# Wider zero products in TensorE's idle time, and a new order for an attention and Fourier-mixing kernel

## The chip, the cores and the metric

The kernel runs on one core of a Trainium2 chip. The core has five engines that work side by side, each through its own queue in order: TensorE (PE; its weight loads are listed as PEld), VectorE (DVE), ScalarE (ACT), GpSimd (POOL) and SyncE (SP), which only issues transfers. The metric is the device time of one execution in microseconds (us), the median over runs. The profile is of one execution and gives its span, from the first to the last instruction.

## The reference, cut to what matters

Chunked attention over four batches of eight heads, then a two-dimensional Fourier transform whose real part is added, a normalisation and a two-layer network with residual:

```python
# attention: q, k, v are (4, 8, 768, 64), mem_k and mem_v (4, 8, 8, 64)
for c in range(S // 32):                       # chunks of 32 queries
    k_ctx = k[:, :, l_start:r_end]             # 16 keys to the left, 8 to the right
    k_full = np.concatenate([mem_k, k_ctx], axis=2)
    v_full = np.concatenate([mem_v, v_ctx], axis=2)
    scores = scale * np.matmul(q_c, k_full.transpose(0, 1, 3, 2))
    a = softmax(scores)
    out[:, :, c_start:c_end] = np.matmul(a, v_full)
# x is (4, 768, 512): the heads side by side
X = np.fft.fft(np.fft.fft(x, axis=1), axis=2)
u = x + np.real(X)
un = (u - mu) / np.sqrt(var + 1e-06)
return u + np.maximum(un @ w_ch1, 0.0) @ w_ch2   # 512 x 2048 and 2048 x 512
```

## The kernel before, in words

Work is cut by batch (`b`, four) and by head pair (`n`, sixteen, four in each batch). For a head pair, q and k are loaded by POOL (`e_load_qk`, L369), v by SP (`e_load_v`, L378 to L387) into the tiles `va`. TensorE transposes q and k in 16 small products each (`turn`, L397; results `trq`, `trk`); ACT copies `trq` out (L415), DVE copies `trk` into the key tile `kTb` (L440). Scores go out in two blocks of twelve products (L453), ACT makes the exponentials (L463), TensorE multiplies with v (L505, tiles `xa` and `xo`), and DVE divides by the sums into `xsb` (L515, L516). There is one bank for scores, so a second block waits for the exponential of the first.

The Fourier transform of a batch is made with tables of sines and cosines as matrix products: rows (L723 and L736 for the first batch, L577 for the others, tile `ps`), then columns (L747, L768, one last row L628, tile `pm`). The tables are made in the kernel: POOL counts (L315, L317), DVE makes angles (L1030 to L1038), ACT the sines (L1177 to L1181), then loads the table of the exponential (L1198). The network's first layer is L885 with the activation L894, its second L903 or, for most parts, L952, which saves products by sums of blocks that DVE makes (L940, tiles `S` and `w_t`) and adds with L957.

Of the first batch's four head pairs the transform needs them all: DVE's folds (L647, L658), POOL's sums of the middle column (L709 to L712, tile `mid`) and DVE's splits into two half-precision parts (L703) stand between the last values and the first row products. L717 is a zero product that clears a bank ahead of L723.

The order in every queue is not written out by hand. `add` records each piece of work as a task with an engine, a cost in microseconds, the tasks that it follows, the buffers that it takes and gives, and a rank. `Plan.order` then goes through planned time and places, on each engine that is free, the ready task of the lowest rank; the program is issued in that order. So a changed cost or rank moves instructions in the queues, on all engines, and semaphores alone decide when they run. `settled(moved)` overwrites the ranks of single tasks, by number, ahead of that.

Zero products: while TensorE is planned idle between the two tasks in `plan.filling`, `order` puts in `e_fill`, a product of the zero tile `dz` into a bank that is given back at the end of the stretch. `FILL` is the cost that is planned for one; TensorE costs count twice in planned time before `WARM`. `t_fill` places the first one. `make_identity` (POOL) and `e_idb` (DVE) make the identity that the transposes need.

Of the kernel before, what the change touches and what calls it, by code (L numbers as in the profile page):

```python
# [13 lines left out]
AFT = mybir.ActivationFunctionType  # L14
# [22 lines left out]
class Plan:  # L37
# [4 lines left out]
    LAG = {"PE": 0.2}  # L42
    OVER = {"DVE": 0.08, "ACT": 0.1}
    FIRST = 45.0
    WARM = 18.0
    SLACK = 0.7
    lead = 0
    ROOM = 1.15
    FILL = 0.17
    filling, fill = None, None  # L50

    def __init__(self, slots):
# [3 lines left out]
    def add(self, engine, cost, emit, after=(), take=(), give=(), rank=None, moved=0.0,  # L56
            loose=False, late=0.0, filler=False, behind=None, lag=0.0, pick=None, grain=0.1, head=1.0, dense=0.15):
        t = dict(engine=engine, cost=cost, emit=emit, after=[a for a in after if a is not None],
                 take=take, give=give, rank=len(self.tasks) if rank is None else rank,
                 moved=moved, done=None, at=None, no=len(self.tasks), loose=loose,  # L60
                 late=late, filler=filler, behind=behind, lag=lag, picks=[pick] if pick else [], grain=grain, head=head, dense=dense)
        self.tasks.append(t)
        return t
# [131 lines left out]
def kernel(  # L195
# [15 lines left out]
    P = 128  # L211
# [766 lines left out]
            nc.sync.dma_start(out[b, HS:HS + 1, :], od[b % 2, 0, 0:1, :])  # L978

    t_zero = add("DVE", 0.2, e_zero, rank=-21)  # L980
    t_table = add("ACT", 1.4, lambda: nc.scalar.activation(warm, zero, AFT.Sin), [t_zero], rank=-3)
    t_iota = add("POOL", 0.7, e_iota, rank=-5)
    t_mkf = add("ACT", 0.2, e_mkf, moved=2.04, grain=0.077, head=6.5)
    t_id = add("POOL", 0.5, lambda: make_identity(nc, ident), rank=-1.5)
    t_scales = add("DVE", 0.2, e_scales, [t_iota], rank=-19)
    t_ones = {}
    def e_idb():
# [4 lines left out]

    t_idb = add("DVE", 0.5, e_idb, [t_id], rank=-16.5)
    t_kz = add("DVE", 0.5, lambda: nc.vector.memset(ks[0][QP:KP], 0.0), rank=-16.95)
    t_kzs = add("POOL", 1.0, lambda: [nc.gpsimd.memset(ks[i][QP:KP], 0.0) for i in range(1, NS)],
                rank=14)
    t_low, LOW = {}, 110
    for i in range(NV):
        e_ = add("DVE" if i < 2 else "POOL", 0.45, lambda i=i: e_edges(i),
                 rank=(-20, -17.3, 17, 17)[i])  # L1000
        t_ones[i] = add("POOL", 0.7, lambda i=i: e_edge_ones(i), [e_], rank=(-3.5, 2, 17.1, 17.1)[i])
        t_low[i] = add("ACT", 1.45, lambda i=i: e_low_rows(i), [t_zero, e_],
                       rank=(0, 1, 2, 3)[i])
    t_masks = add("POOL", 0.86, e_masks, rank=16)
    dz = cpool.tile([P, P], BF16)
    fill_of = []
    t_dz = add("DVE", 0.15, lambda: nc.vector.memset(dz, 0.0), rank=-30)

    def e_fill():
        if not fill_of:  # L1010
            fill_of.append(bank("mlp", [P, 512], FP32, "idle"))
        nc.tensor.matmul(fill_of[0][:, 0:384], dz, strided(dz, 0, [[0, 3], [1, P]]),
                         start=True, stop=True)

    t_fill = add("PE", 0.33, e_fill, [t_dz], take=("mlp",), rank=-1)
    plan.fill = e_fill
    SINES = len(plan.tasks)
    t_kTz = [add("POOL", 0.45, lambda i=i: nc.gpsimd.memset(kTb[i][:, :, 0:MEM0], 0.0), rank=3)
# [5 lines left out]
    tabD = [(yD, rD, kk, sv[:, 0:1], svD[:, 0:1])]  # L1024
    t_angle = {}
    ANG = dict(S=-18, D=-10)
    for nm, parts, y, r, NN, c in (("S", tabS, yS.rearrange(fl3), rS.rearrange(fl3), S, 0.8),
                                   ("D", tabD, yD.rearrange(fl2), rD.rearrange(fl2), DM, 0.6)):

        t1 = [add("DVE", 0.37, lambda p_=p_: nc.vector.tensor_scalar(  # L1030
            p_[0], p_[2], p_[4], FSC, ALU.mult, ALU.add), [t_scales], rank=ANG[nm] + 0.1 * i)
            for i, p_ in enumerate(parts)]
        t2 = add("DVE", c, lambda y=y, NN=NN: nc.vector.tensor_scalar(
            y, y, FSC, float(NN), ALU.subtract, ALU.mult), t1, rank=ANG[nm] + 1)
        t3 = [add("DVE", 0.6 if nm == "S" else 0.75, lambda p_=p_: nc.vector.scalar_tensor_tensor(
            p_[1], p_[2], p_[3], p_[0], ALU.mult, ALU.subtract), [t2], rank=ANG[nm] + 2 + 0.1 * i)
            for i, p_ in enumerate(parts)]
        t_angle[nm] = add("DVE", c, lambda y=y, r=r: nc.vector.scalar_tensor_tensor(  # L1038
            y, r, -1.0, r, ALU.mult, ALU.max), t3, rank=ANG[nm] + 3)
# [160 lines left out]
        t_low[i]["behind"] = t_exp[i - 2, 1]  # L1200
        t_low[i]["rank"] = t_exp[i - 2, 1]["rank"] + 0.1
    t_neg = add("DVE", 0.6, e_negatives, [t_sines], rank=100)
    t_rows = add("DVE", 1.0, e_table_rows, [t_sines, t_neg], rank=101)
    t_idh = add("DVE", 0.25, lambda: nc.vector.tensor_copy(ident_h, ident), [t_id], rank=140)


# [14 lines left out]
    def first_fourier():  # L1221
        t_rest, t_mid, t_row, t_rows_, pre, seen, t_lo = {}, {}, {}, {}, {}, [], ([], [])
        both = None
        for g in range(2):
# [28 lines left out]
            for par in range(2):  # L1253
                for ab in range(2):
                    end = (ab, g) == (1, 1)
                    if g == 0:
                        ff = add("DVE", 0.5,
                                 lambda par=par, ab=ab, g=g: g_ff(par, ab, g, 1),
                                 [pre[par, ab, g], t_norm[3, g]])
                    else:  # L1260
                        ff = add("DVE", 0.55, lambda par=par, ab=ab: g_both(par, ab),
                                 pre[par, ab, 1][:2] + (seen + [pre[p, a, 1][2] for p in range(2) for a in range(2)]
                                                        if (par, ab) == (1, 1) else []),
                                 give=("dn",) if (par, ab) == (1, 1) else ())
                        seen.append(ff)
                    if (par, ab, g) == (0, 0, 1):
                        t_mark.append(ff)
                    hi = add("ACT", 0.5, lambda par=par, ab=ab, g=g: g_hi(par, ab, g),
                             [ff] + (pre[par, ab, 1][2:] if g == 1 else [pre[par, ab, 2]]),
                             take=(("hl",), ("hT",))[par] if (ab, g) == (0, 0) else ())  # L1270
                    lo = add("DVE", 0.48, lambda par=par, ab=ab, g=g: g_lo(par, ab, g),
                             [hi] + (t_lo[par] if end else []), give=("fold",) if end else ())
                    t_lo[par].append(lo)
                    if (par, ab, g) == (0, 0, 0):
                        plan.filling = (t_sc[0, 0], add("PE", 0.0, lambda: let_go(fill_of[0]), [lo],
                                                        give=("mlp",)))
                    tag = ("acc", "mlp")[par]
                    mid_ = (par, ab) == (0, 1)
                    rw = add("PE", 1.0, lambda par=par, ab=ab, g=g: g_rows(par, ab, g),
                             [lo, t_neg, t_rows_.get((par, ab))] + ([t_row[g]] if mid_ else [])  # L1280
                             + ([t_rows_[par, 0]] if end else []),
                             take=(tag,) if g == 0 and not mid_ else (),
                             give=(("hl",), ("hT",))[par] if end else ())
                    t_rows_[par, ab] = rw
                    if g == 1:
                        up = add("ACT", 0.6, lambda par=par, ab=ab: e_up(0, par, ab), [rw],
                                 take=("up",))
                        t_rest[par, ab] = add("DVE", 0.6,
                                              lambda par=par, ab=ab: e_rest(0, par, ab), [up],
                                              give=(tag,))  # L1290
# [260 lines left out]
    for b in range(B):  # L1551
# [3 lines left out]
    t_lv[15]["behind"] = t_x2[TURNED - 1]  # L1555

    moved = {
# [6 lines left out]
        262: 135.01, 269: 1.00059e+06, 275: 396.87, 280: 185.16, 290: -124.87, 318: -83.04, 359: 134.87,  # L1564
# [4 lines left out]
    }  # L1569
    with tc.manual_schedule():  # L1570
        for t in plan.settled(moved):
# [31 lines left out]
```

## Time and profile before

| | us |
|---|---|
| three runs | 276.18, 277.38, 277.41 |
| their median | 277.38 |
| the profiled execution | 276.81 |
| its span | 275.1 |
| TensorE busy | 258.2 (94%) |
| DVE busy | 206.1 (75%) |
| ACT busy | 160.3 (58%) |
| POOL busy | 80.4 (29%) |

A busy TensorE is not one at its peak, since matmuls are pipelined and their ends are modelled. In the timeline a line gives the start in microseconds, the time that the piece took, engine, source line, operation, the tile written and those read, shapes and the number of instructions; the bracket gives the idle time of the engine before it and what ended that. In the rows of merged products the time runs to the modelled end of the last one, so steps from one start to the next are the surer measure. The time of an execution is longer than its span by what lies around the first and last instruction, here 276.81 - 275.1 = 1.7 us.

### The profile page before, as it was taken

How to read it: one execution, taken by the hardware profiler on the slowest of the kernel's cores; microseconds unless marked ns; L12 is line 12 of the kernel's file. 1: busy time of each engine (PE TensorE's matmuls, PEld its weight loads, DVE VectorE, ACT ScalarE, POOL GpSimd, SP SyncE). 2: the span in 40 equal slices, each digit the busy share in tenths (PEclk: the TensorE clock that was granted, in tenths of full speed). 3: DMA queues.
4: the chain of work that ended last, by engine and by line, in shares of the span. 5: the costliest groups of instructions: out<-in, count | busy, mean ns of one | idle time of the engine just before them, and what ended most of it. 6: DMA issues, size and time to landing. Idle time of an engine off the chain costs nothing.

```text
span 275.1 us, 8156 instructions
## 1 busy us (share of the span) xinstructions
PE 258.2 (94%) x3365; PEld 211.5 (77%) x3365; DVE 206.1 (75%) x460; ACT 160.3 (58%) x300; POOL 80.4 (29%) x146
## 2 busy tenths in 40 slices
PE   0299999999999999999999989999999999999995
PEld 0278688788766679767768878888889889888884
DVE  7988997942336999899997996649998868444444
ACT  6598557777764779625935746737164374715150
POOL 8872382241111028025208346001100171100000
PEclk9999999999999999999999999999999999999999
DMA  6997999999999979994599967644942127313152
GB/s 107 202 182 121 175 157 206 197 196 197 195 185 240 235 100 239 170 153 113 186 165 250 176 101 134 141 92 163 133 166 38 41 50 164 89 49 76 66 89 76
DMA packets 116117, 39.98 MB, mean 145 GB/s; under 512 B 104560, under 2 KB 111472, under 8 KB 116080
## 3 DMA queue, kind: packets, MB, share of 16 engines
q1 hardware_dynamic: 93888, 23.54, 46.6%
q0 software_dynamic: 21472, 15.21, 33.8%
q10 hardware_dynamic: 720, 0.72, 0.8%
q8 instruction: 26, 0.43, 0.7%
q14 instruction: 11, 0.09, 0.1%
HBM read 37.36 MB, written 13.37 MB: 184 GB/s over the span
## 4 chain that ended last, share of the span: by engine, by line
PE 78%; DVE 13%; ACT 2%; DMA 2%; issue 2%; SPq 1%; POOL 1%; POOLq 0%; DVEq 0%
PE ph L885 25%; PE pc L952 14%; PE pc L903 10%; PE ps L577 6%; PE xa L505 5%; PE xo L505 3%; PE pm L747 3%; PE ps L736 3%; DVE S L940 2%; PE trk L397 2%; PE trq L397 2%; DMA va<-in_mem_v_dram 2%; DVE xsb L516 1%; PE sc L476 1%; PE sc L453 1%
## 5 line engine op out<-in xcount | busy, mean ns | idle before, releaser
L885 PE MATMUL ph<-unT,w_sb 128*128 128x256 f16 x768 | 89.3, 273 | 0.0
L885 PEld LDWEIGHTS <-w_sb 128*128 128x128 f16 x768 | 73.8, 98 | 10.1 <-issue 0.6
L894 ACT ACTIVATE hT<-ph 128x512 f16<-128x512 f32 x96 | 55.5, 600 | 40.9 <-PE ph L885 17.2
L952 PEld LDWEIGHTS <-hT 128*128 128x128 f16 x320 | 30.9, 98 | 4.7 <-issue 0.8
L952 PE MATMUL pc<-w_sb,hT 128*128 128x256 f16 x256 | 31.9, 273 | 0.3 <-DVE xsb L957 0.3
L957 DVE TENSOR_TENSOR xsb<-pc,xsb 128x256 f32<-128x256 f32 x57 | 23.6, 420 | 9.3 <-PE pc L952 7.9
L903 PE MATMUL pc<-w_sb,hT 128*128 128x512 f16 x128 | 29.7, 380 | 0.0
L488 ACT ACTIVATE e<-sc,mbias 128x192 f32<-128x192 f32 (+1 forms) x48 | 18.8, 491 | 5.4 <-PE sc L476 5.4
L903 PEld LDWEIGHTS <-hT 128*128 128x128 f16 x128 | 11.9, 98 | 12.9 <-issue 0.2
L940 DVE TENSOR_TENSOR S<-hT 128x768 f16<-128x768 f16 (+1 forms) x16 | 8.1, 506 | 16.6 <-ACT hT L894 16.3
L463 ACT ACTIVATE e<-sc,mbias 128x384 f32<-128x384 f32 x32 | 17.0, 581 | 3.6 <-PE sc L453 3.6
L820 DVE BATCH_NORM_STATS2 st<-xsb 128x6 f32<-128x512 f32 x24 | 16.6, 692 | 2.6 <-POOL xsb L808 2.0
L589 ACT CAST up<-ps 128x386 f16<-128x386 f32 x16 | 9.7, 608 | 13.6 <-PE ps L577 12.0
L834 ACT ACTIVATE un<-xsb,rs 128x512 f16<-128x512 f32 x16 | 12.6, 811 | 8.4 <-POOL rs L849 8.4
L952 PE MATMUL pc<-w_t,S 128*128 128x256 f16 x128 | 15.8, 273 | 1.3 <-DVE xsb L957 0.7
L808 POOL TENSOR_TENSOR xsb<-mix,xr 128x512 f32<-128x512 f32 x6 | 8.2, 1368 | 28.0 <-ACT mix L802 24.1
L505 PEld LDWEIGHTS xa<-va,e 128*64 128x64 f32 x384 | 13.1, 143 | 3.8 <-issue 3.0
L505 PE MATMUL xa<-va,e 128*64 128x65 f32 x384 | 15.4, 232 | 0.0
L952 PEld LDWEIGHTS <-S 128*128 128x128 f16 x128 | 12.4, 98 | 3.3 <-issue 1.1
L505 PE MATMUL xo<-va,e 128*64 128x65 f32 x384 | 14.2, 224 | 0.0
L369 POOL DMA_DIRECT2D qs<-in_q_dram x12 | 7.8, 651 | 21.8 <-PE trq L397 18.8
L620 POOL DMA_DIRECT2D xr<-x_back x3 | 2.3, 773 | 37.8 <-ACT up L589 14.2
(189 smaller groups left out, 488.7 us busy)
## 6 DMA issues: line engine op xcount, KB each, us to landing
va<-in_v_dram SPq DMA_DIRECT2D x32, 220.0 KB
w_sb<-in_moe_w_ch_dram POOLq DMA_DIRECT2D x8, 512.0 KB, 15.6
out_dram<-xsb SPq DMA_DIRECT2D x12, 256.0 KB
ks<-in_k_dram POOLq DMA_DIRECT2D x12, 192.0 KB, 6.2
qs<-in_q_dram POOLq DMA_DIRECT2D x12, 192.0 KB, 6.4
x_rows<-xsb POOLq DMA_DIRECT2D x3, 768.0 KB, 4.9
xr<-x_back POOLq DMA_DIRECT2D x3, 768.0 KB, 5.6
out_rows<-xsb SPq DMA_DIRECT2D x9, 256.0 KB
```

Source lines behind the costliest of these rows:

```text
L463: nc.scalar.activation(e1[:, :, :, ts(half, 32)], sc[:, :, 0:6, ts(half, 32)], AFT.Exp, bias=mbias[:, half:half + 1], scale=1.0 / math.sqr ...
L488: nc.scalar.activation(to, src, AFT.Exp, bias=mbias[:, half:half + 1], scale=1.0 / math.sqrt(D))
L505: nc.tensor.matmul(xa[64 * half:64 * half + 64, st, hh, 0:65], e1[:, hh, t6, :], v1[:, hh, 6 * g + t6, 0:65], start=True, stop=True)
L577: nc.tensor.matmul(out_[:, sp, :], part[:, ab, sp * 3 + st, c0:c1], tab[:, sp, st, :], start=(st == 0 and i == 0), stop=(st == 2 and i == 1))
L820: nc.vector.bn_stats(st6, xs[b][:, kt, :])
L834: nc.scalar.activation(un, xs[b][:, kt, :], AFT.Identity, bias=rs[:, 1:2], scale=rs[:, 0:1])
L885: nc.tensor.matmul(ph[:, k, :], w1_sb[:, dt, ts(HH * k + i, P)], unT_of[b, j][:, dt, :], start=(dt == 0), stop=(dt == NDT - 1))
L894: nc.scalar.activation(hT_of[b, j][:, :, i, :], ph, AFT.Relu, bias=0.0, scale=1.0 if (b, j) in FAST else -1.0)
L903: nc.tensor.matmul(pc_of[b, j, r], hT_of[b, j][:, k, i, ts(r, P)], w2_sb[:, HH * k + i, :], start=(i + k == 0), stop=(i + k == HH))
L940: nc.vector.tensor_tensor(out_[:, lo:hi], a[:, lo:hi], c[:, lo:hi], op)
L952: nc.tensor.matmul(pc_of[key], a[:, i, :], w[:, i, :], start=(i == 0 and new), stop=(i == HH - 1), skip_group_check=not new)
L957: nc.vector.tensor_tensor(u, pc, u, ALU.add)
```

## The change

The zero product is made 512 columns wide instead of 384, and its planned cost goes from 0.17 to 0.215 us. The stretch in which it may be placed begins with the first zero product itself instead of the first score block. The planner's `WARM`, up to which TensorE costs count twice, goes from 18 to 6 us of planned time. Costs of tasks of the first microseconds are set anew, and the list of overwritten ranks is replaced by another one of 74 entries. What is computed is the same.

```diff
-    WARM = 18.0
+    WARM = 6.0
...
-    FILL = 0.17
+    FILL = 0.215
...
-    t_table = add("ACT", 1.4, lambda: nc.scalar.activation(warm, zero, AFT.Sin), [t_zero], rank=-3)
+    t_table = add("ACT", 1.55, lambda: nc.scalar.activation(warm, zero, AFT.Sin), [t_zero], rank=-3)
...
-    t_mkf = add("ACT", 0.2, e_mkf, moved=2.04, grain=0.077, head=6.5)
-    t_id = add("POOL", 0.5, lambda: make_identity(nc, ident), rank=-1.5)
+    t_mkf = add("ACT", 1.3, e_mkf, moved=2.04, grain=0.077)
+    t_id = add("POOL", 0.7, lambda: make_identity(nc, ident), rank=-1.5)
...
-    t_kzs = add("POOL", 1.0, lambda: [nc.gpsimd.memset(ks[i][QP:KP], 0.0) for i in range(1, NS)],
+    t_kzs = add("POOL", 2.0, lambda: [nc.gpsimd.memset(ks[i][QP:KP], 0.0) for i in range(1, NS)],
                 rank=14)
...
-        e_ = add("DVE" if i < 2 else "POOL", 0.45, lambda i=i: e_edges(i),
+        e_ = add("DVE" if i < 2 else "POOL", 0.68, lambda i=i: e_edges(i),
...
-    t_dz = add("DVE", 0.15, lambda: nc.vector.memset(dz, 0.0), rank=-30)
+    t_dz = add("DVE", 0.15, lambda: nc.vector.memset(dz, 0.0), rank=-1e7)
...
-        nc.tensor.matmul(fill_of[0][:, 0:384], dz, strided(dz, 0, [[0, 3], [1, P]]),
+        nc.tensor.matmul(fill_of[0], dz, strided(dz, 0, [[0, 4], [1, P]]),
                          start=True, stop=True)

-    t_fill = add("PE", 0.33, e_fill, [t_dz], take=("mlp",), rank=-1)
+    t_fill = add("PE", 0.33, e_fill, [t_dz], take=("mlp",), rank=-1e7)
...
-    for nm, parts, y, r, NN, c in (("S", tabS, yS.rearrange(fl3), rS.rearrange(fl3), S, 0.8),
-                                   ("D", tabD, yD.rearrange(fl2), rD.rearrange(fl2), DM, 0.6)):
+    for nm, parts, y, r, NN, c in (("S", tabS, yS.rearrange(fl3), rS.rearrange(fl3), S, 1.36),
+                                   ("D", tabD, yD.rearrange(fl2), rD.rearrange(fl2), DM, 0.77)):
...
-        t1 = [add("DVE", 0.37, lambda p_=p_: nc.vector.tensor_scalar(
+        t1 = [add("DVE", 0.5, lambda p_=p_: nc.vector.tensor_scalar(
...
-        t2 = add("DVE", c, lambda y=y, NN=NN: nc.vector.tensor_scalar(
+        t2 = add("DVE", 0.95 if nm == "S" else 0.6, lambda y=y, NN=NN: nc.vector.tensor_scalar(
...
-    t_rows = add("DVE", 1.0, e_table_rows, [t_sines, t_neg], rank=101)
+    t_rows = add("DVE", 1.6, e_table_rows, [t_sines, t_neg], rank=101)
...
-                        plan.filling = (t_sc[0, 0], add("PE", 0.0, lambda: let_go(fill_of[0]), [lo],
+                        plan.filling = (t_fill, add("PE", 0.0, lambda: let_go(fill_of[0]), [lo],
                                                         give=("mlp",)))
...
     moved = {
-        2: -99.48, 6: 239.93, 8: -20.42, 10: 9.2, 16: 42.33, 18: 31.86, 25: 21.27, 29: 3, 36: 128.29,
...
+        2: -217.28, 10: -121.19, 13: -133.11, 42: -259.5, 43: -245.91, 59: -155.16, 90: -146.74,
+        141: 229.07, 152: 2.67, 165: 91.92, 174: 11.71, 182: 230.38, 187: 220.03, 194: 252.64,
...
     }
```

In the built program TensorE's queue holds 63 zero products instead of 21, and the same work otherwise. Its first entries, before and after (products, line, tiles):

```
before                              after
 1 L1012 idle<-dz 128x384           15 L1012 idle<-dz 128x512
 1 L1165 mps<-ident_b,mkb           16 L397 trq<-ident_b,qs
16 L397 trk<-turn_b,ks               5 L1012 idle<-dz 128x512
16 L397 trq<-ident_b,qs              1 L1165 mps<-ident_b,mkb
16 L397 trk<-turn_b,ks              16 L397 trk<-turn_b,ks
12 L453 sc<-qT,kTb                   9 L1012 idle<-dz 128x512
16 L397 trq<-ident_b,qs             16 L397 trk<-turn_b,ks
 1 L1012 idle<-dz 128x384            2 L1012 idle<-dz 128x512
16 L397 trk<-turn_b,ks              16 L397 trq<-ident_b,qs
12 L453 sc<-qT,kTb                  12 L453 sc<-qT,kTb
                                    10 L1012 idle<-dz 128x512
                                    12 L453 sc<-qT,kTb
```

On POOL the loads of the first q and k stand ahead of the iota, and the memset of the other two `ks` tiles (L995) behind the loads up to the fourth q. On DVE the memset of the first `ks` tile (L994) stands ahead of the angles, `e_idb` behind the first L1035, and the copy L1204 behind the key tiles of the first two head pairs. On ACT the first L415 stands ahead of the sines.

More of the change, by code (lines that the diff above doesn't have):

```diff
@@ L1557 @@
     moved = {
[6 rows of a table removed]
-        262: 135.01, 269: 1.00059e+06, 275: 396.87, 280: 185.16, 290: -124.87, 318: -83.04, 359: 134.87,
[4 rows of a table removed]
[12 rows of a table added]
     }
```

19 rows, old and new, of the table moved are left out of this document.

## The prediction

> **What bounds the kernel now.** I read the busy table with the slices, then a table of windows, then the timeline of the first 34 us, engine by engine, and last the waits of TensorE behind it. The windows say that two regimes follow each other (columns: stretch, length, then busy time and instructions of PE, weight loads, DVE, ACT, POOL, granted clock, DMA):
>
> ```profile
> PEclk9999999999999999999999999999999999999999
> 0.00:10.00 10.00, 0.50 (x1) 0.10 (x1) 8.40 (x25) 4.99 (x5) 9.07 (x17) 1.00 0.85 135
> 10.00:20.00 10.00, 7.80 (x144) 6.10 (x146) 9.26 (x26) 9.51 (x15) 7.77 (x29) 1.00 1.06 190
> 20.00:30.00 10.00, 9.88 (x243) 7.92 (x239) 8.08 (x20) 8.37 (x17) 2.28 (x4) 1.00 0.85 131
> 60.00:80.00 20.00, 20.00 (x372) 16.17 (x371) 6.16 (x16) 13.27 (x23) 2.61 (x4) 1.00 1.21 196
> ```
>
> From about 33 us on, TensorE is filled and sets the end: whatever brings its dense work forward, or takes a wait out of it, shortens the span one for one. Before that, DVE, ACT and POOL are filled and TensorE waits. The clock row says full speed everywhere, but the durations of one and the same instruction do not:
>
> ```profile
> 1.04 0.50 PE L1012 MATMUL idle<-dz 128*128 128x384 bf16 x1 [1.04 <-DVE zero L310]
> 11.78 0.27 PE L1165 MATMUL mps<-ident_b,mkb 128*128 128x128 bf16 x1 [10.24 <-DVE ident_b L988]
> 16.12 0.88 PE L397 MATMUL trk<-turn_b,ks 100*64 100x100 bf16 x16
> 18.40 0.82 PE L1012 MATMUL idle<-dz 128*128 128x384 bf16 x2
> 24.52 0.53 PE L397 MATMUL trq<-ident_b,qs 96*64 96x96 bf16 x16
> 31.67 1.48 PE L1012 MATMUL idle<-dz 128*128 128x384 bf16 x8
> 32.98 0.33 PE L717 MATMUL ps<-dz 128*128 128x386 bf16 x1
> 33.30 0.24 PE L723 MATMUL ps<-cosS,mid 128*1 128x193 f16 x1
> ```
>
> Sixteen transposes take 0.88 us at 16 us and 0.53 at 24.5. Two zero products fill 18.40 to 19.15 (0.375 each), eight fill 31.67 to 32.98 (0.164 each). So TensorE runs at about half speed until some 22 us, and the clock row does not show it. The first real row product, L723 at 33.30, is my marker for the start of the dense regime. It hangs on other engines:
>
> ```profile
> 14.44 1.28 ACT L1198 ACT_TABLE_LOAD   x1
> 15.84 1.04 ACT L463 ACTIVATE e<-sc,mbias 128x384 f32<-128x384 f32 x2
> 17.48 1.05 ACT L463 ACTIVATE e<-sc,mbias 128x384 f32<-128x384 f32 x2
> 24.45 0.20 DVE L515 RECIPROCAL zs<-xa 128x6 f32<-128x6 f32 x1
> 31.58 0.56 DVE L516 TENSOR_TENSOR xsb<-xa,zs 128x384 f32<-128x384 f32 x1
> L1030 DVE TENSOR_SCALAR yS<-tri,svS x3: 421/455/1189, 2.5 to 3.2; 128x386 f32<-128x386 f32 x3
> 3.11 2.15 POOL L995 MEMSET ks<- 4x1024 bf16 x2
> ```
>
> From 24.45 to 32.14 DVE has no gap; POOL's mid sums follow and end in L723. Before that ACT runs from exponential to exponential, and the first of them waits for the sine tables and the table load. The row of L1030 (least, median, greatest in ns) shows one of three equal operations at 1.19 us: it ran while POOL's memset of 2.15 us did.
>
> **The lead-in, step by step.** In the built order the zero products are 63 instead of 21, with 15 ahead of the first transposes and ten between the first two score blocks. Prices of one: 512 columns are 4/3 of 384, so 0.164 x 4/3 = 0.22 us at full speed and 0.375 x 4/3 = 0.50 at half.
>
> (1) *DVE's tables.* POOL now issues two loads first (0.89 + 0.65 us as at 1.53 and 2.42), so the iota ends at 3.11 instead of 1.57 and DVE's L330 starts at 3.15 instead of 2.27: +0.88. Taken out of DVE's way: the ks memset (0.48 and a gap, 0.52), which now fits in that idle time, the copy L1204 (0.15 net) and the collision (1.19 - 0.45 = 0.74), as the POOL memset stands far later. Net -0.53: DVE is through with the angles and ident_b at 11.5 instead of 12.01. Against it, ident_b is now asked for at about 6 us, and POOL has six edge operations and the identity to do before: it may hold DVE up to 1.0. So 11.5 to 12.5.
>
> (2) *First exponential.* The sines of the columns need the last angle; two activations (12.04 to 13.27: 1.23) and the table load with its warm-up (14.44 to 15.84: 1.4, 1.45 with the hand-over) follow. The query copy (0.80) that stood between now precedes the sines. 11.5 + 0.1 + 1.23 + 1.45 = 14.3, up to 15.3, against 15.84.
>
> (3) *Second exponential.* It needs the second score block, which stands behind ten zero products (2.2 us) and the first block. That in turn waits for the second key's transposes, and these for POOL's ks memset, now behind seven loads. POOL's sum from 3.11: 0.65 + two edge groups at 0.59 + identity 1.09 + load 0.65 + two kTb memsets 1.0 + three loads 1.9 + memset 2.15 = 11.7, or 13.2 if the edge groups wait for DVE as at 8.87 (1.25 + 0.73 there). Transposes 0.48, two zero products 0.44, transposes 0.47 make 13.1 to 14.6; blocks and zero products 0.3 + 2.2 + 0.3 make 15.9 to 17.4. ACT itself is free at (2) + 1.64. So the second exponential comes at 15.95 to 17.4, against 17.48: gain 0.1 to 1.5, I take 0.8 (middle).
>
> (4) *To the first value block's end.* From 17.48 to zs at 24.45 it takes 6.97 now. At full clock: ACT to the next copy 0.94, to the next exponential 1.40, to the end of the query copy 1.70, transposes 0.47, values 0.87, hand-overs 0.10: 5.5. Gain 1.4; the cold rows make the difference (values 1.50 at 19.65 against 0.87 at 23.55).
>
> (5) *DVE to L723.* The same operations as 24.45 to 32.14, but one key copy L440 (1.26) that stood before them now stands among them: -1.25.
>
> Sum: 0.8 + 1.4 - 1.25 = 0.95; 0.25 to 1.65 by the ends of (3). The 42 added products cost nothing as far as they lie in TensorE's waits. That cover is thin: from 7.3 us to L717 the real work is 8 x 0.47 + 8 x 0.28 + 8 x 0.8 = 12.4, the 48 zero products 10.5, of some 25. Idle time is no longer there to catch up in, which is why (3) carries POOL's delay through.
>
> **The dense regime.** No product is added behind L717; the 74 ranks only move work. TensorE's waits there that a move can take are these:
>
> ```profile
> 161.66 0.39 PE L952 MATMUL pc<-w_t,S 128*128 128x256 f16 x2 [0.59 <-DVE S L940]
> 162.52 0.71 PE L952 MATMUL pc<-w_t,S 128*128 128x256 f16 x5 [0.47 <-DVE xsb L957]
> 194.20 1.03 PE L952 MATMUL pc<-w_t,S 128*128 128x256 f16 x8 [0.24 <-DVE xsb L957]
> ```
>
> Start to start against the usual step they are 0.63, 0.75 and 0.40, 1.78 in all; the others (0.39 at L723, 0.47 at 242 us, four under 0.2) stand in both orders. At the first place the new order has the six L628 products (0.75) ahead of the S products and eight L768 (0.55) in their middle: 1.30 of 1.38 covered. At the second a row block L577 (1.01) stands ahead: 0.40 covered. So up to 1.7. Moved work can open new waits: one as large as the largest here, 0.75, is the lower end (-0.75); I take 1.4, nearer the covered sum, as both covers stand in the order itself.
>
> **Sum.** 0.95 + 1.4 = 2.35. The profiled execution took 276.81 (span 275.1, 1.7 around it): 274.5. The median of the three runs, 277.38, is 0.57 above it, so I forecast 277.38 - 2.35 = 275.0.
>
> [...] TensorE worked from 11.78 on, yet at 21.08 twelve score products still took 0.50 instead of 0.35: over 9 us of transposes and small products did not raise the clock. [...]
>
> **Rivals.** (a) *All of it comes*: both ends, 1.65 + 1.8, 277.38 - 3.45 = 273.9. For it: DVE and POOL collide less. Against: two loads ahead of the iota.
> (b) *The lead-in gives nothing, the waits half*: POOL's edge groups are held by DVE, ident_b and the ks memset come late, and the zero products carry it on: 0 + 0.7, 276.7. For it: 1.25 and 0.73 us rows of POOL where 0.18 is usual.
> (c) *The clock is lost again* between 9 and 14 us, where TensorE waits for POOL's memset. Then transposes take 0.64 a block, and ten zero products 5.0 instead of 2.2. With that memset late (13.2): 13.2 + 0.64 + 1.0 + 0.64 + 0.43 + 5.0 = 20.9 for the second score block, the exponential at 21.3 against 17.48: -3.8. If the ten products bring the clock back, (4) keeps its 1.4, (5) its -1.25, the dense regime 1.4: -2.25 in all, 279.6. It decides for slower once more than eight zero products behind the first score block run at half speed (8 x 0.28 = 2.2, all of the gain). For it: the long cold stretch of the profile. Against: nine zero products stand in that gap.
> (d) *Zero products do not raise the clock at all*, so the change does not do what it says: (c) from the start, and in (4) some 0.9 of the 1.4 is lost too: 280.5. Against: the clock did rise in a stretch with zero products; that stretch does not separate them from the value products.
>
> **How the numbers follow.** Forecast 47%, (a) 14%, (b) 22%, (c) 11%, (d) 6%. Half a percent, 1.4 us, is about what can be told from no change: the forecast and (a) are faster, 61%; (b) is the same, 22%; (c) and (d) are slower, 17%. The forecast's own range is 274.3 to 275.9. The range goes down to 273.0, below (a) by the runs' spread toward 276.18, and up to 278.4, through (b) and a first part of (c).
>
> **What would show it.** Right: transposes at about 0.5 us from the first block, first exponential near 14.8, second near 16.7, zs near 22.2, L723 near 32.3, and the three waits at 161 to 194 us gone. Wrong: zero products at 0.5 us behind 9 us, ident_b later than 7.5, POOL's ks memset ending past 13.2, or a new wait of a microsecond among the L952 products.

## Result and profile after

| | before | after |
|---|---|---|
| median | 276.97 (7 runs, 276.18 to 277.41) | 278.79 (7 runs, 278.41 to 280.38) |
| ratio to before | | 1.0084, interval 1.0056 to 1.0112 |
| the profiled execution, its span | 276.81, 275.1 | 279.74, 278.0 |
| first exponential | 15.84 | 17.04 |
| second exponential | 17.48 | 19.38 |
| zs of the second pair | 24.45 | 25.21 |
| L723, the first row product | 33.30 | 35.60 |
| L717 to the start of the last product | 238.67 | 239.23 |

Slower by 0.8%, where 0.9% faster was forecast. The span grew by 2.9 us: 2.3 ahead of L723 and 0.6 behind it. Both parts had been forecast as gains, of 0.95 and 1.4.

The windows of the changed kernel (columns as before) show that the change did what it says. TensorE is busy from the first microseconds:

```profile
0.00:10.00 10.00, 5.95 (x34) 2.58 (x35) 6.78 (x24) 4.75 (x5) 8.26 (x22) 1.00 0.81 133
10.00:20.00 10.00, 8.48 (x117) 4.18 (x116) 9.73 (x25) 8.05 (x14) 7.41 (x24) 1.00 1.19 193
```

5.95 us of 10 in place of 0.50, and DVE's busy time in that first stretch fell from 8.40 to 6.78: the engine that all waited for was kept waiting itself. TensorE's timeline says by whom:

```profile
1.05 4.93 PE L1012 MATMUL idle<-dz 128*128 128x512 bf16 x15 [1.05 <-DVE zero L310]
8.98 0.53 PE L397 MATMUL trq<-ident_b,qs 96*64 96x96 bf16 x16 [3.00 <-DVE ident_b L988]
...
16.45 0.35 PE L453 MATMUL sc<-qT,kTb 64*128 64x64 bf16 x12 [0.45 <-DVE kTb L440]
16.73 2.33 PE L1012 MATMUL idle<-dz 128*128 128x512 bf16 x10
18.99 0.35 PE L453 MATMUL sc<-qT,kTb 64*128 64x64 bf16 x12
...
35.60 0.58 PE L723 MATMUL ps<-cosS,mid 128*1 128x193 f16 x5
```

The transposes take 0.53 us from the first block on (0.88 for sixteen at 16 us before), so the zero products do raise the clock; the trace's record of the granted clock begins at 4.16 us with full speed, against 22.62 before (the clock column of the windows counts the time ahead of that as 1.00). But TensorE then waits 3.00 us for `ident_b`. POOL's timeline and DVE's, side by side, show why:

```profile
1.36 0.88 POOL L369 DMA_DIRECT2D qs<-in_q_dram  x1 [0.86 <-POOLq L1588]
2.25 0.64 POOL L369 DMA_DIRECT2D ks<-in_k_dram  x1
2.99 0.60 POOL L315 IOTA tri<- 128x512 f32 x1
...
5.21 0.75 POOL L342 TENSOR_SCALAR_AFFINE_SELECT va<-va 32x2 f32<-32x2 f32 x1
6.03 0.60 POOL L344 TENSOR_SCALAR_AFFINE_SELECT va<-va 32x2 f32<-32x2 f32 x1
...
7.12 0.29 POOL masks.py:199 TENSOR_SCALAR_AFFINE_SELECT ident<-ident 128x128 f32<-128x128 f32 x1
7.41 0.65 POOL L369 DMA_DIRECT2D qs<-in_q_dram  x1
8.05 0.80 POOL L1018 MEMSET kTb<- 128x384 bf16 x2
...
10.68 1.92 POOL L995 MEMSET ks<- 4x1024 bf16 x2
```

```profile
3.72 0.17 DVE L330 TENSOR_SCALAR svS<-sv 128x3 f32<-128x3 f32 x1 [0.95 <-POOL sv L317]
...
7.44 1.49 DVE L988 CAST ident_b<-ident 128x128 bf16<-128x128 f32 x1 [0.86 <-POOL ident masks.py:199]
...
11.63 1.26 DVE L1030 TENSOR_SCALAR tri<-tri,svD 128x512 f32<-128x512 f32 x1
...
14.18 0.69 DVE L1038 SCALAR_TENSOR_TENSOR tri<-tri 128x512 f32<-128x512 f32 x1
...
15.14 1.25 DVE L440 COPY kTb<-trk 128x1056 bf16<-128x1056 bf16 x1
```

Two loads stand ahead of the iota and the first starts at 1.36, so `sv` comes at 3.69. Two edge groups, the second at 0.75 and 0.60 where the first took 0.18 and 0.24, stand ahead of the identity, which is there at 7.41. The cast of it takes 1.49 us, ending 0.08 after POOL's two memsets (8.85), and the L1030 of the column table takes 1.26, ending 0.28 after POOL's `ks` memset (12.60). In the kernel before these took 0.22 and 0.51:

```profile
5.03 0.51 DVE L1030 TENSOR_SCALAR tri<-tri,svD 128x512 f32<-128x512 f32 x1
...
10.90 0.69 DVE L1038 SCALAR_TENSOR_TENSOR tri<-tri 128x512 f32<-128x512 f32 x1
11.51 0.22 DVE L988 CAST ident_b<-ident 128x128 bf16<-128x128 f32 x1
```

The angles end at 14.87 instead of 11.60, and ACT follows them:

```profile
15.64 1.28 ACT L1198 ACT_TABLE_LOAD   x1
...
17.04 1.03 ACT L463 ACTIVATE e<-sc,mbias 128x384 f32<-128x384 f32 x2
...
19.38 1.05 ACT L463 ACTIVATE e<-sc,mbias 128x384 f32<-128x384 f32 x2 [0.62 <-PE sc L453]
```

In the dense regime the waits that ended at 161.66, 162.52 and 194.20 are gone (one of 0.20 stands at 198.95), and a larger one stands at 149.9. The waits (who waited for whom, us in total, times, longest) and the chain that ended there:

```profile
DVE xsb L516 <- DMA out_dram<-xsb: 4.4, 1, 4.4
...
PE ph L885 <- DVE xsb L516: 2.2, 1, 2.2
```

```profile
142.91 7.95 DMA out_dram<-xsb
...
150.99 0.56 DVE xsb L516
...
152.29 1.91 PE ph L885 x16
```

The last store of the first batch lands 7.95 us after its issue. L516 writes a new tile into the `xsb` buffer that the store reads, so it waits for that. The first layer's L885 needs what L516 gives free, and TensorE stands for 2.41 us, counted start to start against the usual step. SyncE's queue shows where the store stood, first after, then before:

```profile
139.00 0.80 SPq L378 DMA_DIRECT2D va<-in_v_dram  x2
...
140.25 2.57 SPq L858 DMA_TRANSPOSE unT<-un  x2
142.91 1.00 SPq L966 DMA_DIRECT2D out_dram<-xsb  x1
```

```profile
129.33 2.51 SPq L858 DMA_TRANSPOSE unT<-un  x2
131.93 0.53 SPq L966 DMA_DIRECT2D out_dram<-xsb  x1
136.28 0.59 SPq L615 DMA_DIRECT2D x_back<-x_rows  x1
```

In both orders the store, the sixth of `out_dram`, follows two transposing transfers. In the order before, the three stand ahead of the `x_back` transfers and the v loads; in the new order they stand behind these, and the store is issued 11 us later. DVE, on the other hand, is ready for L516 at 146.62; in the order before L516 starts at 150.34 and waits for nothing. The transposing transfers land late as well: by the trace's semaphore updates the second, which L885 reads, at 149.82, just ahead of TensorE.

### The profile page after: what moved, and what is told of

Read it like the earlier page. It is cut to its first block, busy times and chain, and to the rows that moved or that the text cites. A ratio compares the mean times of both kernels' runs of the same rounds, so it can differ in the third digit from the quotient of the medians.

```text
span 278.0 us, 8223 instructions
## 1 busy us (share of the span) xinstructions
PE 266.3 (96%) x3407; PEld 212.3 (76%) x3407; DVE 203.8 (73%) x460; ACT 160.5 (58%) x300; POOL 76.9 (28%) x146
## 4 chain that ended last, share of the span: by engine, by line
PE 69%; DVE 18%; ACT 3%; POOL 3%; DMA 3%; issue 2%; POOLq 0%; DVEq 0%
PE ph L885 26%; PE pc L952 16%; PE pc L903 5%; PE xa L505 4%; PE ps L577 3%; DMA out_dram<-xsb 3%; PE xo L505 3%; PE pm L747 2%; DVE xsb L516 2%; PE ps L736 2%; DVE st L820 2%; PE idle L1012 1%; DVE ff L658 1%; ACT hT L894 1%; PE trq L397 1%
## 5 line engine op out<-in xcount | busy, mean ns | idle before, releaser
L885 PE MATMUL ph<-unT,w_sb 128*128 128x256 f16 x768 | 88.5, 273 | 2.3 <-DVE xsb L516 2.2
L885 PEld LDWEIGHTS <-w_sb 128*128 128x128 f16 x768 | 74.2, 98 | 12.3 <-issue 2.8
L894 ACT ACTIVATE hT<-ph 128x512 f16<-128x512 f32 x96 | 56.1, 599 | 44.0 <-PE ph L885 18.6
L940 DVE TENSOR_TENSOR S<-hT 128x768 f16<-128x768 f16 (+1 forms) x16 | 6.7, 422 | 18.5 <-ACT hT L894 18.1
L1012 PE MATMUL idle<-dz 128*128 128x512 bf16 x63 | 17.9, 411 | 1.0 <-DVE zero L310 1.0
L505 PEld LDWEIGHTS xa<-va,e 128*64 128x64 f32 x384 | 12.5, 137 | 3.7 <-issue 3.3
L505 PE MATMUL xa<-va,e 128*64 128x65 f32 x384 | 14.7, 226 | 0.0
L594 DVE TENSOR_TENSOR up<-ps,up 128x386 f16<-128x386 f32 x16 | 9.6, 598 | 6.1 <-ACT up L589 6.1
L369 POOL DMA_DIRECT2D qs<-in_q_dram x12 | 8.0, 668 | 21.3 <-PE trq L397 16.1
```

The costliest lines, as they stand in the source:

```text
L505: nc.tensor.matmul(xa[64 * half:64 * half + 64, st, hh, 0:65], e1[:, hh, t6, :], v1[:, hh, 6 * g + t6, 0:65], start=True, stop=True)
L885: nc.tensor.matmul(ph[:, k, :], w1_sb[:, dt, ts(HH * k + i, P)], unT_of[b, j][:, dt, :], start=(dt == 0), stop=(dt == NDT - 1))
L894: nc.scalar.activation(hT_of[b, j][:, :, i, :], ph, AFT.Relu, bias=0.0, scale=1.0 if (b, j) in FAST else -1.0)
L1012: nc.tensor.matmul(fill_of[0], dz, strided(dz, 0, [[0, 4], [1, P]]), start=True, stop=True)
```

## Experiments

All but the first start from the changed kernel and edit its finished order: `line` is the list that `settled` returns, a task is named by its number, and `no(n)` is the place of task n. Only the order is edited, or zero products are added and left out; what is computed stays the same. The kernel before had a median of 276.8 to 276.9 beside these runs. Ratios are to it. Each execution's mean granted clock is on record. The shortest stretch at half speed in the profiled executions below is 3.41 us (154.03 to 157.44 without zero products), which takes 0.006 off that mean (0.5 x 3.41 of 278 us), so 0.994 or less is read as a clock lost for at least one such stretch.

**The zero products alone.** The kernel before, its products made 512 wide, and forty of them from the first idle time on:

```diff
+        at = next(i for i, t in enumerate(line) if t.get("no") == 23) + 1
+        line[at:at] = [dict(emit=e_fill)] * 40
```

> The kernel before, in its own order, with 40 zero products of 512 columns put behind its first one, so that TensorE works from 1 to about 12 us. Theory (a full clock is worth the cold rows, about 1.4 us between the second exponential and the first values, and nothing on DVE or ACT is later): transposes at 0.53 us from the first block, L723 at 31.9 instead of 33.30, ratio to the kernel before 0.995 to 0.996. Rival (ACT and DVE hold the lead-in anyway, a warm clock is worth nothing): L723 at 33.0 to 33.4, ratio 0.999 to 1.001.

277.43, ratio 1.0026 (1.0007 to 1.0045). The clock rises at 5.06 and the first two exponentials come at 15.37 and 16.98, each 0.5 us earlier than before, but it is lost again. Its windows and timeline, some lines:

```profile
14.00:18.00 4.00, 2.81 (x75) 2.09 (x75) 3.91 (x13) 3.99 (x8) 3.66 (x11) 1.00 0.75 156
19.00:22.00 3.00, 3.00 (x66) 2.70 (x62) 1.77 (x4) 2.75 (x6) 0.26 (x1) 0.50 1.22 204
```

```profile
16.46 0.35 PE L453 MATMUL sc<-qT,kTb 64*128 64x64 bf16 x12 [0.79 <-ACT e L463]
...
18.76 0.51 PE L453 MATMUL sc<-qT,kTb 64*128 64x64 bf16 x12 [0.55 <-POOL va L347]
19.20 1.57 PE L505 MATMUL xa<-va,e 128*64 128x65 f32 x24
...
31.51 1.90 PE L1012 MATMUL idle<-dz 128*128 128x512 bf16 x8
33.25 0.33 PE L717 MATMUL ps<-dz 128*128 128x386 bf16 x1
```

The granted clock is 0.50 in the stretch from 18.71 to 22.13, though no wait of TensorE in the microseconds ahead of it is longer than 0.79; of the 75 products there (14 to 18 us) 48 were transposes. Eight of the ten executions lost the clock. And the eight products ahead of L717, now a third longer (1.74 us from their start to L717's, for 1.31 before), end past the mid sums that L723 needs (32.82): L723 stands at 33.51, 0.2 later than before. So the zero products alone bring nothing here.

**No zero products at all** in the changed kernel's order, except the first:

```diff
+        line = [t for t in line if "no" in t]
```

> The changed kernel with all zero products but the first taken out; every queue keeps its order. Theory (the order of POOL and DVE makes the lead-in late: iota behind two loads, identity behind the edge operations, two DVE operations held by POOL): the first key tile is copied at about 15.1 as in the changed kernel (12.98 before), and L723 stays at 35 us or later, with a cold TensorE up to 36.5; ratio 1.006 to 1.012. Rival (the zero products themselves, which stand on the chain for 4 us of the lead-in, make it late): L723 at 33.0 to 34.0, ratio below 1.003.

281.27, ratio 1.0139 (1.0093 to 1.0186), an interval that just meets the changed kernel's. The clock rises only at 24.32, yet zs stands at 25.23 (25.21 with them) and L723 at 34.91 (35.60). In the lead-in of these two profiles the products give and take the same. What is lost is lost behind it: the store lands later (152.97 instead of 150.86), the wait at L885 is 4.49 instead of 2.41, and the clock is lost from 154.03 to 157.44. All four executions lost the clock (0.992 to 0.994), two of the seven with the products did. Why the store lands later is not settled.

**Iota and identity ahead of POOL's loads** (tasks 2 and 4 ahead of 42):

```diff
+        for n in (2, 4):
+            line.insert(no(42), line.pop(no(n)))
```

> The changed kernel with two POOL tasks moved to the front: the iota and then the identity ahead of the two first loads; all else in its order, all zero products kept. Theory (POOL's order is what made the tables late): the angles end at about 12.3 us instead of 14.87, the second exponential starts near 17.1 instead of 19.38, L723 near 33.3 instead of 35.60, ratio 1.000 to 1.003. Rival (zero products): the second exponential at 18.5 or later, L723 at 34.6 or later, ratio above 1.004.

275.54, ratio 0.9967 (0.9938 to 0.9996), 3.25 below the changed kernel, with intervals that don't meet, and better than the theory had. DVE's timeline, to be set against that above:

```profile
5.47 0.22 DVE L988 CAST ident_b<-ident 128x128 bf16<-128x128 f32 x1
...
8.47 0.49 DVE L1030 TENSOR_SCALAR tri<-tri,svD 128x512 f32<-128x512 f32 x1
...
10.36 0.69 DVE L1038 SCALAR_TENSOR_TENSOR tri<-tri 128x512 f32<-128x512 f32 x1
```

All three losses are gone (L330 stands at 2.80), the angles end at 11.05 and L723 stands at 32.23, 3.4 earlier. Behind that, this profiled execution (279.55) lost the clock at 150.78, after the wait at L885; two of the ten did, and it is not read further.

**The store issued early** (task 702, the last store, right behind 696 on SyncE):

```diff
+        t = line.pop(no(702))
+        line.insert(no(696) + 1, t)
```

> The changed kernel with one SP task moved: the last store of the first batch, from behind a load of v and two transposing transfers to right behind the store ahead of it. Theory (TensorE's new wait of 2.4 us at 150 us is this store's landing, 7.95 us after its issue at 142.91, which DVE's L516 needs for its buffer, and TensorE for the bank that L516 frees): the wait at 150 us gone, ratio 1.000 to 1.003. Rival (the transfers there are late as a whole, and the wait moves to the next of them): a wait of over 1 us between 140 and 160 us remains, ratio above 1.005.

278.88, ratio 1.0082 (1.0049 to 1.0114): no gain. L516 no longer waits, but TensorE still does at the same L885. The view of the waits, 140 to 160 us, puts it down to DVE's sum of weights:

```profile
PE ph L885 <- DVE w_sb L927: 1.2, 1, 1.2
```

That can't be the cause: the queues of TensorE and DVE are those of the changed kernel, and there this L885 starts at 152.29, ahead of L927 at 153.38. The trace's semaphore updates show another: the second transposing transfer `unT<-un`, issued at 144.89, lands at 152.88, and L885 starts 0.14 us later, at 153.01. In the five profiled executions below that have the store early, L885 starts 0.14 us after this landing too. So it is the rival's mechanism: the wait moved to the next late transfer. Without this wait, 1.2, the 238.53 from L717 to the last product would be 237.4. This execution also shows the prediction's rival (c), in TensorE's timeline:

```profile
8.99 0.53 PE L397 MATMUL trq<-ident_b,qs 96*64 96x96 bf16 x16 [1.81 <-DVE ident_b L988]
...
12.00 0.88 PE L397 MATMUL trk<-turn_b,ks 100*64 100x100 bf16 x16
12.81 4.02 PE L1012 MATMUL idle<-dz 128*128 128x512 bf16 x9
```

The clock is at half from 10.0 to 16.82, nine zero products take 4.02 us instead of 2.12, the second exponential comes at 21.18 and L723 at 37.12. Three of the six executions lost the clock.

**Identity right behind the iotas, loads still first** (task 4 ahead of 59):

```diff
+        line.insert(no(59), line.pop(no(4)))
```

> The changed kernel with one POOL task moved: the identity right behind the iota, ahead of the third load and the edge operations; the two loads stay ahead of the iota. Theory (the identity is the larger part: DVE's 0.86 us of waiting for it and the 1.27 us that its copy was then held by POOL): the four copies end at about 6.8 instead of 9.1 us, the second exponential starts near 17.2, L723 near 33.2, ratio 0.999 to 1.003. Rival (the iota behind the loads is the larger part): L723 at 34.4 or later, ratio above 1.005.

278.53 (276.54 to 280.12), ratio 1.0053 (1.002 to 1.0085). The profiled execution is the fastest of them, 276.54: angles at 12.00, L723 at 32.62, 3.0 earlier than in the changed kernel. Four of the ten lost the clock and took 279.03 to 280.12; the six others took 276.54 to 279.38, with a median of 277.0.

**The mended POOL order without zero products**, the first excepted:

```diff
+        for n in (2, 4):
+            line.insert(no(42), line.pop(no(n)))
+        line = [t for t in line if "no" in t]
```

> The kernel with iota and identity first, and all zero products but the first taken out. Theory (with POOL's order mended the zero products are worth the warm clock): a cold TensorE until after 20 us, L723 at 33 us or later against 32.23 with them, ratio 0.004 or more above that kernel's 0.9967. Rival (what they give by the clock they take by standing in the queue): L723 at 31.8 to 32.6, ratio 0.994 to 0.999.

279.99, ratio 1.0118 (1.0081 to 1.0155), 4.45 above the same order with them. Again not by the lead-in (L723 at 31.67, against 32.23) but at the same place as above: 3.99 at L885, and half a clock from 149.96 to 153.37. All four executions lost the clock (0.988 to 0.994), while eight of the ten with the products kept it; the two that lost it took 278.77 and 279.55. So most of the 4.45 goes with the clock.

**Twelve fewer zero products** around the first score blocks, in the mended POOL order:

```diff
+        zeros = [i for i, t in enumerate(line) if "no" not in t]
+        for i in reversed(zeros[34:46]):
+            line.pop(i)
```

> The kernel with iota and identity first, and twelve of its 63 zero products taken out: six of the ten between the first two score blocks and the six ahead of the first values and of the next query transposes, which stand on its chain. Theory (on the chain each costs its 0.22 us, up to what ACT then holds): the second exponential at about 15.6 instead of 16.43, zs of the second pair at 21.4 instead of 22.26, L723 near 31.4 instead of 32.23, ratio 0.992 to 0.995. Rival (ACT takes over at once): L723 at 32.0 or later, ratio as with all of them, 0.996 to 0.998.

276.75, ratio 0.9999 (0.9974 to 1.0024), with executions from 274.75 to 280.44. The profiled one (274.88) has the second exponential at 15.34 and L723 at 30.77, both over a microsecond earlier; the median has nothing of it. Four of the ten lost the clock, but the six that kept it have a median of 276.6 too, against 275.5 for the eight that kept it with all the products. So no gain is shown.

**Mended POOL order, store early and L927 behind L594**:

```diff
+        for n in (2, 4):
+            line.insert(no(42), line.pop(no(n)))
+        t = line.pop(no(702))
+        line.insert(no(696) + 1, t)
+        t = line.pop(no(735))
+        line.insert(no(443) + 1, t)
```

> The kernel with iota and identity first, the last store of the first batch right behind the one ahead of it on SP, and the last weight sum (L927) on DVE behind the L594 that stood behind it and that frees a bank. Theory (the wait at 148 to 152 us is first the store's landing, then L927 ahead of the freeing): no wait above 0.7 us between 140 and 160 us, the clock kept there, ratio 0.988 to 0.992. Rival (transfers are late as a whole there): a wait of 1 us or more remains in that stretch, ratio 0.995 or above.

275.01, ratio 0.9932 (0.9906 to 0.9959): faster than both kernels. TensorE's waits of this execution, without the three in the first 9 us:

```profile
...
PE ps L736 <- DVE hl L703: 0.2, 1, 0.2
PE pc L952 <- DVE xsb L957: 0.2, 1, 0.2
PE ph L885 <- DMA unT<-un: 0.2, 1, 0.2
```

L723 stands at 31.63, and from L717 to the last product it is 237.49. The 0.2 at L885 is the transposing transfer again. Nothing shows that the move of L927 gave anything; the wait that it was meant for was not L927's.

**The same, repeated:**

> A repetition of the version with iota and identity ahead of the loads, the store and L927 moved: 275.0 again, ratio 0.990 to 0.996, beside the three others on the same chip.

274.85, ratio 0.9921 (0.9896 to 0.9946), and 237.50 from L717 to the last product. This profiled execution (275.41) has L723 1.4 later than its twin, for one transfer that landed later:

```profile
13.81 0.53 PE L397 MATMUL trq<-ident_b,qs 96*64 96x96 bf16 x16 [1.30 <-DMA qs<-in_q_dram]
```

So a microsecond in the lead-in of a single profile is within what a load's landing does by itself.

**The store and L927 moved, POOL's order as changed:**

```diff
+        t = line.pop(no(702))
+        line.insert(no(696) + 1, t)
+        t = line.pop(no(735))
+        line.insert(no(443) + 1, t)
```

> The changed kernel with its own lead-in, but the last store of the first batch issued ahead of the v load and the two transposing transfers on SP, and the weight sum L927 of DVE moved behind L594. Theory (two separate losses: POOL's order costs 3.3 us in the lead-in, the late store 2.4 us at 149.8): the lead-in stays (L723 at 35 to 36), the wait of 2.4 at L885 falls under 0.5, and the time is 278.8 - 2.2 = 276.6, ratio near 0.999. Rival (the wait is repaid elsewhere: TensorE then waits for the next late thing, as with the store alone, 278.9): 278.3 to 279, ratio 1.006. Where the clock is lost in the lead-in, L723 near 37 and 1 to 2 us more, under either theory.

277.59, ratio 1.0046 (1.0023 to 1.0068). Between the two expectations: the wait at L885 is gone, and from L717 to the last product it is 237.41, as the theory had it; L723 at 35.20, as it had it too. By the medians it is 1.2 and not 2.2, and the interval meets that of the changed kernel. Six of the twelve executions lost the clock.

**Store, L927 and the identity alone**, the four lines above and:

```diff
+        line.insert(no(59), line.pop(no(4)))
```

> The same two moves, with the identity right behind the iotas on POOL, but two loads still ahead of the iotas. Theory (of the lead-in's loss the late identity makes about 3 us and the two loads ahead of the iota 0.4 to 1): 278.8 - 2.2 - 2.6 = 274 to 275.5, between the version with both moved (275.0) and 276. Rival (the time hangs on the clock, which a late start of the transposes loses; the identity alone was worth 0.25 in the median though 3.0 in the profile): 276 to 277, with executions scattered over 3 us.

275.53 (274.68 to 276.68), ratio 0.9952 (0.9934 to 0.997), at the upper edge of what the theory gave. By the medians the identity alone is worth 2.1 us; in the profiles L723 comes 2.6 earlier than without it (32.61 for 35.20). The rest to the version with iota and identity first, some 0.6, can't be put down to the two loads alone, since in this profiled execution TensorE stands at L885 for 1.6 us, for the transposing transfer (the chain that ended there):

```profile
140.49 8.46 DMA unT<-un
...
149.09 1.91 PE ph L885 x16
```

**Six zero products in place of ten** between the first two score blocks of the version with POOL's order, store and L927 mended:

```diff
+        zeros = [i for i, t in enumerate(line) if "no" not in t]
+        for i in reversed(zeros[36:40]):
+            line.pop(i)
```

> That version with six zero products in place of ten between the first two score blocks. Theory (the ten, 2.26 us, hold the second score block when its bank has long been free: exponential ends 14.4, block at 15.45): the second block comes 0.8 us earlier, the second exponential at 15.0 to 15.2 instead of 15.84, L723 at 30.9 instead of 31.6, time 274.2 to 274.5, ratio near 0.990. Rival (the products keep the clock, or what follows is bound by ACT and DVE anyway): 275.0 or more, L723 unmoved at 31.6 though the second exponential moved.

274.43, ratio 0.9909 (0.9885 to 0.9934), within the theory's range, but its interval meets that of the same kernel with ten (0.9896 to 0.9946). The second exponential came at 15.34 and L723 at 31.48, half a microsecond later than expected. Here too TensorE stands at L885 for the transposing transfer, 1.5 us, and from L717 to the last product it is 238.65. That these products cost time is likely and not shown.

## Why the prediction was wrong

Its profiled sum was 274.5; the profiled execution took 279.74. Of the 5.24 us between, the lead-in makes 0.95 + 2.30 = 3.25 and the dense regime 1.4 + 0.56 = 1.96.

*Step (1), DVE's tables, failed.* It gave 11.5 to 12.5 and measured was 14.87. Four pieces make it up. `sv` came 0.57 later than the iota's sum said (DVE's L330 at 3.72 for 3.15), 0.46 of it since the first load starts at 1.36 and not where the iota had started, at 0.90. DVE waits 0.86 for the identity. The four casts of it take 1.18 more than before (7.44 to 9.12, for 11.51 to 12.01), and L1030 0.75 more. Together 3.36, on the 11.5 of the sum. The prediction had the second piece ("it may hold DVE up to 1.0"), and it had priced just this kind of collision at 0.74, as a gain, since the `ks` memset would stand far later. It did stand later, and hit another L1030, because DVE was later too. The cast against the kTb memsets was not looked for. The mended order took all of this away and with it 3.4 us of the lead-in and 3.25 of the median, which shows that step (1) was the place.

*Step (2)* followed from the first, with a term that was too long: from the last angle to the first exponential it had 0.1 + 1.23 + 1.45 = 2.78, and 2.17 was measured (14.87 to 17.04). ACT's L1180 started at 14.18, while DVE was still at the last angle, so one of the two activations did not follow it. By luck this hides 0.6 of what step (1) lost.

*Step (3)* had the second exponential 0.8 earlier; it came 1.9 later. The ten zero products did hold it, by the 0.62 that ACT waits, as in its upper case. POOL's `ks` memset, which it feared, ended at 12.60 within its range and held the transposes of nobody: the key copies behind DVE's tables (15.14) came later.

*Step (4)* was right: 5.83 from the second exponential to zs, for 5.5, against 6.97. That the clock would be full by then was an assumption: the profile before has it from 22.62 us on only. In the changed kernel it was there from 4.16. *Step (5)* was right: from zs to L723 it is 10.39, for 8.85 before (24.45 to 33.30) and the moved copy's 1.25, 10.1. In the changed kernel both terms were there, under a later start.

*The dense regime.* The two covers did what they were said to: both waits are gone. The step that failed is the lower bound, "one as large as the largest here, 0.75". The new wait was 2.41, through a queue that it had not followed: a store on SyncE, moved with two transposing transfers behind the `x_back` transfers and the v loads. DVE needs the store's buffer, and TensorE what DVE's L516 gives free. With the store early, 237.41 to 237.50 stand against 238.67 where the transposing transfer landed in time: 1.2 of the 1.4. Where it landed late the part took 238.5 to 239.2, so this transfer is the second half of the same oversight.

*The rivals.* (d) is refuted by the transposes of 0.53. (b) had the mechanism of the lead-in (edge groups held, `ident_b` late) but let it end at no gain, where it cost 2.3. (c) did not happen in the profiled execution of the changed kernel; it did in that of the early store, with the second exponential at 21.18 where (c) had said 21.3.

The clock stays the part that is least settled. The records of the profiled executions with all the early zero products have it rise between 4.0 and 7.0 us, with the first product always at 1.04 or 1.05, and all stretches between two changes are multiples of 3.41 us (13.65 from 5.06 with the zero products alone, 6.83 from 10.0 with the store early, 3.41 from 154.03 without zero products). The length of a wait does not decide whether the clock is lost: it was lost after one of 2.24 us (mended POOL order, at 148) and with none longer than 0.79 ahead of it (zero products alone), while the changed kernel kept it through 2.41. Counted in steps of 3.41 us from the recorded changes, this last wait falls into two steps, in which TensorE was busy for 2.53 and 2.06 us; the wait of 2.24 falls into one, with 1.33. In all the profiles it goes the same way at L885: the clock was kept with 1.95 or more in a step and lost with 1.33 or less. The lead-in does not fit as simply (kept with 1.72, lost with 1.78), so what makes the clock fall stays open.

By the mean clock, the losses go with the two late things. Of the executions with the late identity and the store early, three of six and six of twelve lost it; with an early identity and the late store, six of the twenty that kept all the zero products; with both early, none of 31. The changed kernel lost it in two of seven, and its five others have a median of 278.67, so its slowness is not the clock's.

## What to carry to other kernels

Filling an idle engine changes nothing for the engine that it waits for (here 5.95 us of work in TensorE's first 10, and still a wait of 3.00 for DVE's cast): follow that engine first, and at each piece of work that is moved on a slow queue, ask which operations beside it will now run at the same time (here that cast took 1.49 us instead of 0.22). A store is not done when its inputs are ready (here it landed 7.95 us after its issue); follow the buffer that it holds, from its place in the queue to its landing, to the next writer and to whoever waits for that one. When a wait goes away, look for the next thing to end at the same place: here a store, then a transposing transfer ended at one L885. And test a named releaser against another run with the same order: the weight sum, which the view named, was none.

## What was not expected of the hardware

A cast of 128x128 from float32 on DVE took 0.22 us in the mended order, beside POOL's selects, and 1.49 in the changed kernel, beside a load's issue and two memsets of POOL, ending 0.08 us after these. POOL's 32x2 selects took 0.18 at the least, and 0.75 and 0.60 beside DVE's L1033 and L1035, ending 0.04 and 0.05 us after these; the one of 1.25 in the kernel before ended 0.05 after DVE's L1038. So in these rows each operation that took longer ended at most 0.08 us after one of the other engine. What it waited for the traces do not show: the cast began 0.6 us before the first of the memsets, while a load was being issued, so which of the two made it long is open.
